# First token group of a convolution and MLP kernel: exponential, block B, doubling copy and wake-up moved

## Chip, core and metric

The kernel runs on one core of one Trainium2 chip. The metric is device microseconds of one execution, as the median of several runs. The core has five engines that run side by side: TensorE (matmuls; PE in the profile, its weight loads PEld), VectorE (DVE), ScalarE (ACT), GpSimd (POOL) and SyncE (SP). SyncE only issues transfers (DMA). ScalarE and GpSimd can issue them too, each on a queue of its own, in program order with their other instructions.

## The reference

A dynamic convolution over 16384 tokens (4 sequences of 4096) with 192 features, 8 heads and 7 taps, followed by an MLP with a squared Relu:

```python
w = np.exp(weight_gen - max over the 7 taps)
w = w / (w.sum over the 7 taps + 1e-09)
x_pad = six rows of zeros ahead of each sequence, then x
conv[b, s, h, :] = sum over k of w[b, s, h, k] * x_pad[b, s + k, h, :]
h = conv @ w_in                  # 192 -> 2048
r = np.maximum(h, 0.0)
g = s * (r * r) + b
out = g @ w_out                  # 2048 -> 192
```

## The kernel before, in words

The tokens go in 32 groups of 512. The 2048 hidden features are 16 blocks of 128, handled in pairs as eight chunks; `wc_91` to `wc_98` are the eight converted weight chunks in the listings (chunks 0 to 7 here).

Precision: float32 values are split into a high part in a reduced format (fp32r) and the rest. Products are made of high x high, low x high and high x low, so a group's operands are `xa` and `xb` (two blocks of the 192 features), each with a high half `[:, 0]` and a low half `[:, 1]`. `xb` fills only 64 partitions, and is copied once to the other 64 (the doubling copy, `xb<-xb`), since the matmuls use both halves.

Weights: `load_weights` (L167) brings chunk pairs from DRAM: four transfers of block A (L179), eight small ones of block B (L188) and one of the second weights (L196) per chunk. For the first pair chunk 0 and chunk 1 are loaded by calls of their own. `convert(i)` (L209) splits a chunk in steps, between which other work stands: ScalarE takes Abs (L218, needs the whole raw chunk); VectorE makes three passes (L221, L225, L229); ScalarE casts the high part (L234, reads L229's result); VectorE makes `v` (L236, L240); TensorE adds up six matmuls (L250 to L252), and ScalarE casts the low part (L253). `ahead(i, n)` runs the next n steps of chunk i.

The first group of the program has a convolution of its own (`conv_pieces`, g == 0): softmax of the taps (`softmax_a` L370 on VectorE, `exp` L382 on ScalarE, `softmax_b` L385 on VectorE), then products of `xr` (the group's rows of x) with `w`: the "row tails" (eight products that end in `xb`) and the "row firsts" (eight that end in `xa`). TensorE transposes and sums the products into PSUM (`px`, L320): 28 for the tails, 28 for the firsts. `row_hi` (L353) casts the high half on ScalarE, `row_lo` (L359) makes the low half on VectorE and, for `xb`, issues the doubling copy (L364). `run_pieces(0, a, b)` runs pieces a to b of that list.

TensorE's start: `awake` (L258) runs 48 small matmuls on constants while the first data is fetched. Then come the transposes, and `mm1_pair` (L512) makes the first products of chunk 0: six each of `xa` and `xb`, with the rest of chunk 0's conversion between them.

The order of instructions is written out by hand (`tc.manual_schedule`): each engine runs its own in the order of the program text. Transfers of SyncE and ScalarE count their completion on eight semaphores that they share in turn; a transfer that takes a semaphore again first waits until the one before it on that semaphore has landed. After the first group (from L708) the loop over the other 31 groups keeps TensorE full with `mm1_quad` and `mm2_quad`.

Of the kernel before, what the change touches and what calls it, by code (L numbers as in the profile page):

```python
# [20 lines left out]
def dynamic_conv_then_relu2_mlp(  # L21
# [24 lines left out]
    nc = tc.nc  # L46
# [3 lines left out]
    P = 128  # L50
# [43 lines left out]
    def load_rows(i):  # L94

        t0 = ORDER[i] * T
        wg = xin.tile([P, NT, H, K], F32, tag="wg", name="wg")
        nc.sync.dma_start(
            out=wg.rearrange("p a h k -> p (a h k)"),
            in_=wgf[t0:t0 + T, :].rearrange("(p a) n -> p (a n)", a=NT),  # L100
        )
        xt = rows.tile([P, NT + HALO, D], F32, tag="xr", name="xr")
        src = xf[t0 - HALO:t0 - HALO + 1, :]
        for a0, a1 in ((0, 2 * NT - 1), (2 * NT - 1, NT + HALO)):
            nc.sync.dma_start(
                out=xt[:, a0:a1].rearrange("p a d -> p (a d)"),
                in_=bass.AP(src.tensor, src.offset + a0 * D, [[NT * D, P], [1, (a1 - a0) * D]]),
            )
        xt_t[i], wg_t[i] = xt, wg
# [99 lines left out]
    def convert(i):  # L209


        r = raw_t[i // 2][:, i % 2]
        hi, lo = wc[i][:, 0], wc[i][:, 1]
        low_w, high_w = r[:, :, 0], r[:, :, 1]
        fv = high_w.bitcast(F32)
        t = raw.tile([P, CW], U32, tag="t", name="t", bufs=1)
        tv = t.bitcast(F32)
        nc.scalar.activation(out=tv, in_=fv, func=AF.Abs)  # L218
        yield

        nc.vector.tensor_scalar(  # L221
            out=tv, in0=tv, scalar1=LEAST, scalar2=MOST, op0=ALU.max, op1=ALU.min
        )

        nc.vector.tensor_scalar(  # L225
            out=t, in0=t, scalar1=3, scalar2=0x3FFFFFFF,
            op0=ALU.logical_shift_left, op1=ALU.bitwise_and,
        )
        nc.vector.scalar_tensor_tensor(  # L229
            out=high_w, in0=high_w, scalar=0xC0000000, in1=t,  # L230
            op0=ALU.bitwise_and, op1=ALU.bitwise_or,
        )
        yield
        nc.scalar.copy(out=hi, in_=fv)  # L234

        nc.vector.tensor_scalar(  # L236
            out=t, in0=high_w, scalar1=0xFF800000, scalar2=None, op0=ALU.bitwise_and
        )
        v = raw.tile([P, CW], F32R, tag="v", name="v", bufs=2)
        nc.vector.scalar_tensor_tensor(  # L240
            out=v, in0=low_w, scalar=2.0 ** -52, in1=tv, op0=ALU.mult, op1=ALU.mult
        )
        yield

        ps = ps_h.tile([P, 2, T], F32, tag="h1", name="ph")
        n = CW // 2
        for a in range(2):
            c = slice(a * n, (a + 1) * n)
            o = ps[:, a, 0:n]
            nc.tensor.matmul(out=o, lhsT=eye_f, rhs=fv[:, c], start=True, stop=False)  # L250
            nc.tensor.matmul(out=o, lhsT=neg_eye, rhs=hi[:, c], start=False, stop=False)  # L251
            nc.tensor.matmul(out=o, lhsT=eye, rhs=v[:, c], start=False, stop=True)  # L252
        nc.scalar.copy(out=lo.rearrange("p (a n) -> p a n", a=2), in_=ps[:, :, 0:n])  # L253
        yield
# [3 lines left out]
    def awake():  # L258

        ph = ps_h.tile([P, 2, T], F32, tag="h1", name="ph")  # L260
        for _ in range(48):
            nc.tensor.matmul(out=ph[:, 0, 0:P], lhsT=eye, rhs=ones, start=True, stop=True)  # L262

    def constants():
        nc.gpsimd.memset(ones_f, 1.0)
        nc.vector.tensor_copy(out=ones, in_=ones_f)
        nc.gpsimd.affine_select(
            out=eye_f, in_=ones_f, pattern=[[-1, P]], base=0, channel_multiplier=1,
            compare_op=ALU.is_equal, fill=0.0,
        )  # L270
        nc.vector.tensor_copy(out=eye, in_=eye_f)
        nc.vector.tensor_scalar(
            out=neg_eye, in0=eye_f, scalar1=-1.0, scalar2=None, op0=ALU.mult
        )
# [29 lines left out]
    def conv_pieces(g):  # L304
# [33 lines left out]
        def row_firsts(k0, k1):  # L338
            def f():
                out = st["p"][0][:, k0:k1].rearrange("p k a (q n) -> p k (a q) n", q=Q)  # L340
                times(out[:, :, :, 0:G], 0, k0, k1 - k0, 0, NT * Q, 2, G)
                times(out[:, :, :, G:32], G, k0, k1 - k0, 0, NT * Q, 2, 32 - G)
                for a in range(NT):
                    sum_taps(0, k0, k1, a)
            return f
# [10 lines left out]
        def row_lo(i):  # L356
            def f():
                x = st["x"][i]
                nc.vector.tensor_tensor(  # L359
                    out=x[R[i], 1], in0=st["ps"][i][R[i]], in1=x[R[i], 0].bitcast(F32), op=ALU.subtract  # L360
                )
                if i == 1:
                    b = x.bitcast(F32)
                    nc.sync.dma_start(out=b[P // 2:P], in_=b[0:P // 2])  # L364
                else:
                    xt_t.pop(g)
                    x_t[g] = parts_of(st["x"])
            return f
# [97 lines left out]
        if g == 0:  # L466
            return [
                softmax_a, exp, softmax_b, row_tails(0), row_tails(1), row_tails(2), row_tails(3), row_hi(1),
                row_lo(1), row_firsts(0, 2), row_firsts(2, 4), row_firsts(4, 6), row_firsts(6, 7),
                row_hi(0), row_lo(0),  # L470
            ]
        return [
# [39 lines left out]
    def mm1_pair(n, p, between=None):  # L512

        g, k = divmod(n, NQ)
        new_h(n, p, "h0")
        turns = [(0, (0, 1, 2)), (1, (0, 1, 2))] if between is None else [
            (0, (0, 2)), (1, (0, 2)), (0, (1,)), (1, (1,))
        ]
        left = 6
        for at, (block, cs) in enumerate(turns):  # L520
            if at == 2:
                between()
            for c in cs:
                part, v = x_t[g][block][c]
                left -= 1
                for j, rows in enumerate(HALVES[::-1]):
                    rows = rows if block else slice(0, P)
                    nc.tensor.matmul(  # L528
                        out=h_t[n, p][:, j], lhsT=w1(2 * k + p, part, block, j, rows), rhs=v[rows],
                        start=(at == 0 and c == 0), stop=(left == 0),  # L530
                    )
# [121 lines left out]

    with tc.manual_schedule():
        constants()
        load_rows(0)
        nc.scalar.activation(out=spare, in_=ones_f[:, 0:1], func=AF.Exp)
        load_weights(0, (0,), nc.scalar)
        load_weights(0, (1,))
        load(1)  # L660
        load_weights(1)
        nc.sync.dma_start(out=s_sb, in_=s.partition_broadcast(P))
# [6 lines left out]
                next(parts[i])  # L669

        awake()
        run_pieces(0, 0, 7)
        ahead(0, 1)
        run_pieces(0, 7, 8)
        ahead(0, 1)
        run_pieces(0, 8, 15)
        ahead(0, 1)
        ahead(1, 1)

        beside = ((2, 4), (4, 5), (5, 7), (7, 8), (8, 10), (10, 12), (12, 14), (14, 15))  # L680
# [84 lines left out]
```

## Time and profile before

| | |
|---|---|
| median of 3 runs | 1195.92 us (1195.82 to 1199.31) |
| the profiled execution | 1195.58 us, its span 1193.9 us |
| mean granted TensorE clock over the span | 0.994 |
| busy over the span: TensorE, weight loads, VectorE, ScalarE, GpSimd | 1172.4, 1052.6, 931.9, 825.6, 6.1 us |

Times below count from the span's start. A busy TensorE is one with a matmul in flight, not one at its peak. Transfer issues on a queue (SPq, ACTq) are listed by the time that the issuing took, waits included where they fall between merged issues; when the data has landed is in another view. The granted clock is a share of 2.4 GHz.

### The profile page before, as it was taken

The numbers are of one execution on the slowest core, as the hardware profiler recorded it, in microseconds if no ns is written. First come the engines' busy times: TensorE is split into PE (matmuls) and PEld (weight loads), VectorE is DVE, ScalarE is ACT, GpSimd is POOL, SyncE is SP. The second block draws the span as 40 slices with busy tenths as digits, with TensorE's granted clock in tenths as the row PEclk, the third lists the DMA queues.
The fourth block names the chain that finished last, engine by engine and source line by source line (L and its number), as shares of the span: only waits on it lengthen the run. The fifth ranks groups of instructions, "written<-read, shape, count | busy, mean of one in ns | idle before, by whom it ended". The sixth has DMA issues, their size and how long they took to land.

```text
span 1193.9 us, 30070 instructions
## 1 busy us (share of the span) xinstructions
PE 1172.4 (98%) x12776; PEld 1052.6 (88%) x12776; DVE 931.9 (78%) x1356; ACT 825.6 (69%) x890; POOL 6.1 (1%) x22
## 2 busy tenths in 40 slices
PE   7799999999999999999999999999999999999997
PEld 6578899998999989999899898998989989899897
DVE  5788777788877778887777887777888777888843
ACT  1676677776776767767677676776767767677674
POOL 0000000000000000000000000000000000000000
PEclk9899999999999999999999999999999999999999
DMA  6332222211222221222221222222112222212110
GB/s 148 99 60 41 46 45 33 46 26 34 46 45 44 34 45 25 36 45 46 33 45 28 35 43 46 46 32 46 26 34 46 46 41 37 41 28 37 24 23 15
DMA packets 171370, 50.63 MB, mean 42 GB/s; under 512 B 160228, under 2 KB 163940, under 8 KB 171236
## 3 DMA queue, kind: packets, MB, share of 16 engines
q1 hardware_dynamic: 170980, 48.58, 23.7%
q8 instruction: 100, 1.64, 0.6%
q14 instruction: 34, 0.28, 0.1%
q10 hardware_dynamic: 256, 0.13, 0.0%
HBM read 27.70 MB, written 12.58 MB: 34 GB/s over the span
## 4 chain that ended last, share of the span: by engine, by line
PE 96%; DVE 1%; ACT 1%; DMA 0%; issue 0%; POOL 0%; ACTq 0%; POOLq 0%
PE po L615 47%; PE ph L546 43%; PE po L597 2%; PE ph L528 1%; PE ph L262 1%; PE px L320 1%; PE ph L250 1%; DVE gl L569 0%; DMA xb<-xb 0%; ACT gh L563 0%; ACT r L559 0%; ACT r L557 0%; PE ph L285 0%; PE ph L252 0%; PE ph L251 0%
## 5 line engine op out<-in xcount | busy, mean ns | idle before, releaser
L615 PE MATMUL po<-wc,gh 64*128 64x384 f32 x3936 | 570.8, 356 | 0.0
L615 PE MATMUL po<-wc,gl 64*128 64x192 f32 x3936 | 493.5, 247 | 0.7 <-DVE gl L569 0.7
L569 DVE TENSOR_TENSOR gl<-r,gh 128x1024 fp32r<-128x1024 f32 x256 | 313.0, 1223 | 221.5 <-ACT gh L563 213.1
L557 ACT ACTIVATE r<-ph 128x1024 f32<-128x1024 f32 x256 | 248.8, 1023 | 308.6 <-PE ph L546 303.7
L615 PEld LDWEIGHTS po<-wc,gl 64*128 64x128 f32 x3936 | 375.7, 188 | 6.2 <-DVE gl L569 1.0
L615 PEld LDWEIGHTS po<-wc,gh 64*128 64x128 f32 x3936 | 369.2, 184 | 5.5
L546 PE MATMUL ph<-xa,wc 64*128 64x512 f32 x2976 | 371.0, 394 | 0.0
L546 PEld LDWEIGHTS ph<-xa,wc 64*128 64x128 f32 x2976 | 269.6, 184 | 57.3 <-issue 0.2
L563 ACT CAST gh<-r 128x1024 fp32r<-128x1024 f32 x256 | 268.8, 1050 | 7.9
L559 ACT ACTIVATE r<-r 128x1024 f32<-128x1024 f32 x256 | 271.1, 1059 | 0.3
L546 PE MATMUL ph<-xb,wc 64*128 64x512 f32 x1488 | 193.0, 391 | 0.0
L406 DVE TENSOR_TENSOR pr<-xt,w 128x1536 f32<-128x1536 f32 (+1 forms) x124 | 187.5, 1553 | 1.8 <-DVE w L392 0.6
L546 PEld LDWEIGHTS ph<-xb,wc 64*128 64x128 f32 x1488 | 139.5, 184 | 34.1
L417 DVE TENSOR_TENSOR pr<-pr 128x1536 f32<-128x1536 f32 (+1 forms) x124 | 140.7, 1154 | 2.1
L627 DVE SCALAR_TENSOR_TENSOR u<-po,s_sb,bias 128x192 f32<-128x192 f32 x128 | 49.7, 408 | 1.6 <-PE po L597 1.6
L633 DVE SCALAR_TENSOR_TENSOR y<-po,s_sb,u 128x192 f32<-128x192 f32 x128 | 49.6, 408 | 0.1
L425 DVE TENSOR_TENSOR acc<-pr 128x768 f32<-128x768 f32 x31 | 29.7, 958 | 1.1
L436 DVE STREAM_TRANSPOSE xT<-acc 128x128 f32<-128x128 f32 x124 | 27.6, 280 | 1.0
L441 DVE STREAM_TRANSPOSE xT<-acc 128x128 f32<-128x128 f32 x124 | 26.3, 269 | 0.0
L597 PE MATMUL po<-wc,gh 128*128 128x384 f32 x80 | 24.0, 362 | 0.1
L597 PE MATMUL po<-wc,gl 128*128 128x192 f32 x80 | 20.4, 254 | 1.9 <-DVE gl L569 1.9
L454 DVE TENSOR_TENSOR xa<-xT,xa 128x512 fp32r<-128x512 f32 x31 | 21.2, 684 | 0.0
(55 smaller groups left out, 360.0 us busy)
## 6 DMA issues: line engine op xcount, KB each, us to landing
xt<-in_x_dram SPq DMA_DIRECT2D x120, 132.0 KB, 4.0
out_dram<-y SPq DMA_DIRECT2D x124, 96.0 KB, 1.9
xb<-xb SPq DMA_DIRECT2D x124, 64.0 KB, 2.3
wg<-in_weight_gen_dram SPq DMA_DIRECT2D x124, 28.0 KB, 2.6
r<-in_moe_w_out_dram SPq DMA_DIRECT2D x8, 384.0 KB, 3.7
r<-in_moe_w_in_dram SPq DMA_DIRECT2D x12, 128.0 KB, 2.8
r<-in_moe_w_in_dram SPq DMA_DIRECT2D x24, 32.0 KB, 2.6
xr<-in_x_dram SPq DMA_DIRECT2D x1, 672.0 KB
```

What stands on the lines that cost most here:

```text
L406: nc.vector.tensor_tensor(out=pr[:, k0:k1, :, h * G:(h + 1) * G], in0=bass.AP(xs.tensor, xs.offset, [xs.ap[0], [FQ, n], [FQ, J], [1, G]]), ...
L417: nc.vector.tensor_tensor(out=pr[:, o:o + n], in0=pr[:, o:o + n], in1=pr[:, a:a + n], op=ALU.add)
L425: nc.vector.tensor_tensor(out=acc, in0=pr[:, 0], in1=pr[:, 2], op=ALU.add)
L546: nc.tensor.matmul(out=h_t[n, p][:, j], lhsT=w1(2 * k + p, part, block, j, rows), rhs=v[rows], start=(at < 2 and c == 0), stop=(at >= 4 an ...
L557: nc.scalar.activation(out=r[p], in_=h_t.pop((n, p)), func=AF.Relu)
L559: nc.scalar.activation(out=r[p], in_=r[p], func=AF.Square)
L563: nc.scalar.copy(out=gh, in_=r[p])
L569: nc.vector.tensor_tensor(out=gl, in0=sq, in1=gh.bitcast(F32), op=ALU.subtract)
L597: nc.tensor.matmul(**m)
L615: nc.tensor.matmul(**m)
L627: nc.vector.scalar_tensor_tensor(out=u[i], in0=o_t[g][tiles[i]][:, 1, :], scalar=s_sb, in1=bias, op0=ALU.mult, op1=ALU.add,)
L633: nc.vector.scalar_tensor_tensor(out=y[:, t], in0=o_t[g][t][:, 0, :], scalar=s_sb, in1=u[i - 1], op0=ALU.mult, op1=ALU.add,)
```

## The change

Five edits, all in the first 50 us:

- The dummy exponential on `spare`, which loads ScalarE's table, stands ahead of `load_rows(0)`.
- Block B of chunks 0 and 1 (16 transfers of 16 KB) is issued from GpSimd; before, chunk 0's eight were ScalarE's and chunk 1's eight SyncE's.
- The doubling copy of `xb` is issued from ScalarE, not SyncE.
- `awake` runs four float32 matmuls on `wg` (224 columns), not 48 on constants, and so waits for `wg` to land.
- Order of the first group: the cast of the high weights stands one step earlier; `row_firsts(0, 2)` stands ahead of `row_lo(1)`; the last `ahead` of chunk 0 ahead of `row_lo(0)`; and the products with a high x high part of both blocks stand ahead of the conversion, the other eight behind it.

```diff
         )
+        nc.scalar.copy(out=hi, in_=fv)
         yield
-        nc.scalar.copy(out=hi, in_=fv)
...
         ph = ps_h.tile([P, 2, T], F32, tag="h1", name="ph")
-        for _ in range(48):
-            nc.tensor.matmul(out=ph[:, 0, 0:P], lhsT=eye, rhs=ones, start=True, stop=True)
+        w = wg_t[0].rearrange("p a h k -> p (a h k)")
+        for _ in range(4):
+            nc.tensor.matmul(out=ph[:, 0, 0:NT * H * K], lhsT=eye_f, rhs=w, start=True, stop=True)
...
-                    nc.sync.dma_start(out=b[P // 2:P], in_=b[0:P // 2])
+                    nc.scalar.dma_start(out=b[P // 2:P], in_=b[0:P // 2])
...
-                row_lo(1), row_firsts(0, 2), row_firsts(2, 4), row_firsts(4, 6), row_firsts(6, 7),
+                row_firsts(0, 2), row_lo(1), row_firsts(2, 4), row_firsts(4, 6), row_firsts(6, 7),
...
-            (0, (0, 2)), (1, (0, 2)), (0, (1,)), (1, (1,))
+            (0, (0,)), (1, (0,)), (0, (2, 1)), (1, (2, 1))
...
         constants()
+        nc.scalar.activation(out=spare, in_=ones_f[:, 0:1], func=AF.Exp)
         load_rows(0)
-        nc.scalar.activation(out=spare, in_=ones_f[:, 0:1], func=AF.Exp)
-        load_weights(0, (0,), nc.scalar)
-        load_weights(0, (1,))
+        load_weights(0, (0,), nc.gpsimd)
+        load_weights(0, (1,), nc.gpsimd)
...
         awake()
-        run_pieces(0, 0, 7)
+        run_pieces(0, 0, 2)
         ahead(0, 1)
-        run_pieces(0, 7, 8)
+        run_pieces(0, 2, 8)
         ahead(0, 1)
-        run_pieces(0, 8, 15)
+        run_pieces(0, 8, 14)
         ahead(0, 1)
+        run_pieces(0, 14, 15)
         ahead(1, 1)
```

ScalarE, from its first instruction to the cast of chunk 0's low weights; before, then with the change (`e` is the softmax's input, `r` a raw weight chunk, `t` its absolute value, `px` the transposed sums):

```order
L657 ACT_TABLE_LOAD
L657 ACTIVATE spare<-ones_f 128x1
L188 DMA r<-in_moe_w_in_dram 16x256 x8
L383 ACTIVATE e<-e 128x224
L218 ACTIVATE t<-r 128x768
L353 CAST xb<-px 64x512
L353 CAST xa<-px 128x512
L234 CAST wc_91<-r 128x768
L218 ACTIVATE t<-r 128x768
L253 CAST wc_91<-ph 128x768
```

```order
L657 ACT_TABLE_LOAD
L657 ACTIVATE spare<-ones_f 128x1
L384 ACTIVATE e<-e 128x224
L218 ACTIVATE t<-r 128x768
L354 CAST xb<-px 64x512
L233 CAST wc_91<-r 128x768
L365 DMA xb<-xb 64x1024
L354 CAST xa<-px 128x512
L218 ACTIVATE t<-r 128x768
L253 CAST wc_91<-ph 128x768
```

The eight transfers ahead of the exponential are gone, the cast of the high weights has moved ahead of xa's, and the doubling copy stands between the two. The second Abs is chunk 1's, ahead of the cast L253 of chunk 0 in both.

VectorE, from the row tails to the first pass over chunk 1 (`pr` are the products, `w` the softmax); before, then with the change:

```order
L310 TENSOR_TENSOR pr<-xr,w 128x7x2x16 x8
L221 TENSOR_SCALAR t<-t 128x768
L225 TENSOR_SCALAR t<-t 128x768
L229 SCALAR_TENSOR_TENSOR r<-r,t 128x768
L359 TENSOR_TENSOR xb<-px,xb 64x512
L310 TENSOR_TENSOR pr<-xr,w 128x32x24
...
L359 TENSOR_TENSOR xa<-px,xa 128x512
L236 TENSOR_SCALAR t<-r 128x768
L240 SCALAR_TENSOR_TENSOR v<-r,t 128x768
L221 TENSOR_SCALAR t<-t 128x768
```

```order
L311 TENSOR_TENSOR pr<-xr,w 128x7x2x16 x8
L221 TENSOR_SCALAR t<-t 128x768
L225 TENSOR_SCALAR t<-t 128x768
L229 SCALAR_TENSOR_TENSOR r<-r,t 128x768
L311 TENSOR_TENSOR pr<-xr,w 128x32x24
L311 TENSOR_TENSOR pr<-xr,w 128x32x8
L360 TENSOR_TENSOR xb<-px,xb 64x512
...
L236 TENSOR_SCALAR t<-r 128x768
L240 SCALAR_TENSOR_TENSOR v<-r,t 128x768
L360 TENSOR_TENSOR xa<-px,xa 128x512
L221 TENSOR_SCALAR t<-t 128x768
```

Two row firsts now stand ahead of xb's low half, and `v` ahead of xa's.

TensorE, from the wake-up to the second chunk's conversion; before, then with the change:

```order
L262 MATMUL ph<-ones,eye 128x128 x48
L320 MATMUL px<-eye_f,pr 64x128 x28
L320 MATMUL px<-eye_f,pr 128x128 x28
L528 MATMUL ph<-xa,wc_91 128x512 x4
L528 MATMUL ph<-xb,wc_91 128x512 x4
L250 MATMUL ph<-r,eye_f 128x384
...
L528 MATMUL ph<-xa,wc_91 128x512 x2
L528 MATMUL ph<-xb,wc_91 128x512 x2
```

```order
L263 MATMUL ph<-wg,eye_f 128x224 x4
L321 MATMUL px<-eye_f,pr 64x128 x28
L321 MATMUL px<-eye_f,pr 128x128 x28
L529 MATMUL ph<-xa,wc_91 128x512 x2
L529 MATMUL ph<-xb,wc_91 128x512 x2
L250 MATMUL ph<-r,eye_f 128x384
...
L529 MATMUL ph<-xa,wc_91 128x512 x4
L529 MATMUL ph<-xb,wc_91 128x512 x4
```

Four products instead of eight stand ahead of the conversion (L250 and the five behind it), eight instead of four behind it.

## Rows read from the trace of the kernel before

**Rows 1.** Stretches: from:to, length, busy us (instructions) of PE, PEld, DVE, ACT, POOL, clock, DMA, GB/s.

```profile
0.00:17.00 17.00, 15.27 (x73) 14.47 (x74) 7.25 (x20) 2.78 (x4) 0.76 (x6) 1.00 0.49 146
17.00:33.00 16.00, 6.64 (x37) 5.62 (x35) 11.11 (x19) 2.83 (x4) 0.00 (x0) 0.81 0.80 169
...
95.00:1180.00 1085.00, 1084.26 (x12312) 981.89 (x12310) 860.03 (x1242) 773.79 (x830) 5.30 (x16) 1.00 0.23 37
```

**Rows 2.** Chain of waits, 0 to 60 us: start us, us, what.

```profile
20.12 4.93 PE px L320 x28
...
25.07 0.59 ACT xa L353
...
29.27 4.67 DMA xb<-xb
...
33.98 1.22 PE ph L528 x4
35.20 1.58 PE ph L250 x2
...
38.42 0.05 ACT wc L253
...
49.17 2.37 PE po L597 x15
```

**Rows 3.** Waits, 0 to 50 us: us in total, times, longest us.

```profile
PE ph L528 <- DMA xb<-xb: 6.3, 1, 6.3
```

**Rows 4.** Timeline: start us, us, instruction, [idle before it, what ended that].

```profile
1.05 1.32 ACTq L188 DMA_DIRECT2D r<-in_moe_w_in_dram  x3
1.08 0.34 POOL L267 TENSOR_SCALAR_AFFINE_SELECT eye_f<-ones_f 128x128 f32<-128x128 f32 x1
...
2.40 5.98 ACTq L188 DMA_DIRECT2D r<-in_moe_w_in_dram  x5
...
3.38 0.39 DVE L377 TENSOR_TENSOR e<-wg,mx 128x224 f32<-128x224 f32 x1
8.42 0.39 ACT L383 ACTIVATE e<-e 128x224 f32<-128x224 f32 x1 [6.12 <-DMA r<-in_moe_w_in_dram]
...
10.29 2.50 DVE L310 TENSOR_TENSOR pr<-xr,w 128x224 f32<-128x224 f32 x8
11.10 3.66 SPq L188 DMA_DIRECT2D r<-in_moe_w_in_dram  x8
...
12.28 0.90 ACT L218 ACTIVATE t<-r 128x768 f32<-128x768 f32 x1 [3.47 <-DMA r<-in_moe_w_in_dram]
...
14.41 0.96 DVE L229 SCALAR_TENSOR_TENSOR r<-r,t 128x768 uint32<-128x768 uint32 x1
...
18.18 0.68 DVE L359 TENSOR_TENSOR xb<-px,xb 64x512 fp32r<-64x512 f32 x1 [2.82 <-ACT xb L353]
18.79 4.35 DVE L310 TENSOR_TENSOR pr<-xr,w 128x768 f32<-128x768 f32 x8
...
26.88 0.96 DVE L240 SCALAR_TENSOR_TENSOR v<-r,t 128x768 fp32r<-128x768 uint32 x1
...
39.89 0.90 ACT L218 ACTIVATE t<-r 128x768 f32<-128x768 f32 x1
```

**Rows 5.** SyncE's own waits, 0 to 50 us: us in total, times, longest us.

```profile
SPq L179 <- DMA xr<-in_x_dram: 4.4, 1, 4.4
```

**Rows 6.** Weight loads by shape, 0 to 55 us: busy us, mean ns, idle before.

```profile
L262 PEld LDWEIGHTS ph<-ones,eye 128*128 128x128 f32 x48 | 10.3, 332 | 1.7 <-DVE eye L271 1.7
...
L528 PEld LDWEIGHTS ph<-xa,wc 128*128 128x128 f32 x18 | 3.1, 188 | 4.1 <-ACT wc L253 2.1 <-ACT wc L234 1.7
```

**Rows 7.** DMA issues, 0 to 60 us: count, KB each, median us to landing.

```profile
r<-in_moe_w_out_dram SPq DMA_DIRECT2D x6, 384.0 KB, 3.7
...
r<-in_moe_w_in_dram ACTq DMA_DIRECT2D x8, 16.0 KB, 4.9
r<-in_moe_w_in_dram SPq DMA_DIRECT2D x8, 16.0 KB, 1.9
```

## The prediction

> **What bounds the kernel now.** I read the stretches first. In the long middle (95 to 1180 us) TensorE is busy 1084.26 of 1085 us, so nothing but its own work sets the time there [rows 1], and none of that work is edited. In 17 to 33 us it is busy 6.64 of 16. A gain can only come from the first 50 us, and whatever starts the continuous TensorE work earlier shortens the whole kernel by as much.
>
> Then the chain of waits through that start [rows 2]. It runs through the wake-up, the transposes of the first group, and the doubling copy of xb (4.67 us); only then come the products, the conversion matmuls of chunk 0 and, at 38.42, the copy L253 that ends this conversion. I call that moment T. From T on ScalarE's order is the same in both kernels, so I count everything up to T.
>
> The waits name the biggest hole: TensorE waits 6.3 us for xb<-xb [rows 3]. Its issue at 29.27 is late because it stands at the end of SyncE's list, although VectorE had finished xb at 18.86 [rows 2, 4]. The second hole is earlier. ScalarE issues eight 16 KB transfers before the exponential; these take from 1.05 to 8.38, so the exponential starts at 8.42 though its input was ready at 3.77 [rows 4]. SyncE itself stands 4.4 us in the middle of chunk 0's weights, waiting for xr [rows 5].
>
> The clock: the view prints 1.00 for the first 17 us [rows 1], but a 128x128 weight load takes 332 ns in the wake-up against 188 ns in the products [rows 6]. I therefore take the lower level (1.2 GHz) for the wake-up: its 48 matmuls did not bring the higher one while they ran.
>
> **The change, part by part**, against the profiled execution (1195.58 us, span 1193.9; the median of the runs shown is 1195.92, which is 0.34 more).
>
> *Exponential.* It can start at 3.8. From its start in the trace to the first row tail is 1.87 us (8.42 to 10.29), so the tails could start at 5.7 [rows 4]. They then wait for xr, which landed by 10.3 at the latest (in the trace they waited for nothing). With their 2.50 us they end between 8.2 and 12.8.
>
> *Block B on GpSimd.* No row shows a GpSimd transfer. The nearest row is the same eight transfers from ScalarE, 7.3 us or 0.92 us each [rows 4]. The lower bound is SyncE's eight in 3.66 us, 0.46 each; for the upper I let each issue cost a whole issue-to-landing of 16 KB, 1.9 us [rows 4, 7]. I take 0.92. GpSimd is free at 1.42, so chunk 0's eight are issued by 8.8; with 2.6 us to land (between 1.9 and 4.9 [rows 7]) they are there at 11.4, and chunk 1's eight at 18.7 (1.4 + 16 x 0.92 + 2.6). The Trainium skill ("DMA: Bandwidth & Descriptors", Specifications) gives about 1 us to the first byte for this path against 0.6 for the other two. With 1 us per issue, an estimate from that page, everything below would come 0.6 us later; no run here shows it.
>
> *SyncE's list.* It loses eight block-B issues (3.66 us) and the doubling copy. SyncE's and ScalarE's transfers share eight completion semaphores, and a ninth waits until the one before it on its semaphore has landed. With block B gone, wg, two parts of xr, four of block A and chunk 0's second weights are just eight: of the 4.4 us stall nothing stays ahead of them. The last is issued near 4 instead of behind the stall, lands by 9 with 4.9 us, and does not decide. Chunk 0 begins at 11.4 (12.28 in the trace).
>
> *From chunk 0 to T.* Abs L218 to the end of L229: 3.1 us as in the trace (12.28 to 15.37) [rows 4], so 14.5 (15.0 if the tails end at 12.8). VectorE then does the eight firsts (4.35) with xb's low part (0.6) behind the second: 19.5. The first two took 1.3 (18.79 to the transposes' start at 20.12 [rows 2, 4]), so xb is ready at 16.4. TensorE's last four transposes (4.93 / 28 = 0.18 each [rows 2]) end at 20.2, ScalarE's xa copy (0.6) at 20.8; beside it VectorE makes v (L236 and L240, the longer 0.96) by 21.4 [rows 2, 4]. The hi copy L234 is now earlier on ScalarE, behind L229, hidden by the firsts. Then four products instead of eight stand before the conversion, 1.22 / 4 = 0.3 each [rows 2]: 22.0. The conversion itself takes 3.2 (35.20 to 38.42 [rows 2], mostly at the lower clock). **T = 25.2 instead of 38.42: 13.2 us less.**
>
> *Doubling copy on ScalarE.* Issued at about 16.4, when VectorE has xb, it lands at 21.1 if it keeps its 4.67, and is wanted at 21.4. It is hidden by the firsts and the xa copy, with 0.3 us of cover; without it each us late costs a us. Behind it on ScalarE stands only the xa copy, which starts 3.8 us later.
>
> *Wake-up.* Four float32 matmuls of 224 columns, once wg has landed, before 3.4. The pair L250 of 384 columns took 1.58 [rows 2], so each is at most 0.92 and all end by 7.1, where the 48 end at about 12 (1.7 + 10.3 [rows 6]). The tail transposes, paced by the tails or at 0.18 each, then end by 13 at the latest. The xb copy (0.6) that waits for them stands behind Abs (ends 12.3) and its reader runs at 15.7: hidden, over 2 us of cover. If the clock rises sooner, the conversion saves up to half of its 3.2.
>
> *Order of the products.* Four more products stand behind T. Two (xa's low part) run while L253 works; the others may delay the first Relu by 0 to 0.5 us. I take 0.
>
> *Chunks 1 to 3.* Abs of chunk 1 would run at 21.4; its data is there at 18.7, 2.7 us of cover. Chunk 2 is wanted 1.5 us behind T (39.89 against 38.42 [rows 2, 4]), at 26.7. SyncE had issued it before the doubling copy at 29.3 [rows 2], and its list gets 8.1 us shorter (3.66 + 4.4): 21.2 at the latest, and with 3.7 us to land [rows 7] 24.9, 1.8 us of cover.
>
> Sum: 13.2 us off 1195.58 is 1182.4, and against the median **1182.7 us**.
>
> **The rivals.**
>
> *GpSimd is slow (slower).* Abs of chunk 1 stands ahead of L253 on ScalarE. With p us per issue chunk 1 is complete at 1.4 + 16p + 2.6, and Abs adds 0.9. T passes 38.42 once p is over 2.1 us. At 2.5 T is 44.9 and the time 1202. For it: no row prices this queue. Against it: 2.1 is more than any whole 16 KB transfer of SyncE's took, by the median [rows 7]. Chance 0.06.
>
> *GpSimd in between (no change).* From p = 1.9 to 2.3 the result lies within 3.6 us of before, 0.3%, about what a measurement can tell from no change; at 1.9 T is 35.3 and the time 1192.8. Chance 0.07.
>
> *GpSimd's issues stop while VectorE works (still faster).* In the trace GpSimd has nothing to do beside VectorE here, so nothing speaks against it. The tails' 2.50 us [rows 4] then delay chunk 0 to 13.9. Some four of chunk 1's issues fit into VectorE's wait for Abs, the other four follow when v is made at 21.4 + 2.5 = 23.9: chunk 1 at 23.9 + 3.7 + 2.6 = 30.2, Abs ends at 31.1, so 7.3 us gained instead of 13.2: 1188.6. The Trainium skill has such a rule, against this change ("SBUF — State Buffer", SBUF: two separate sides): GpSimd cannot write descriptors while VectorE runs in a mode that takes both ports, and it advises the other queues. By that page the tails, which read two tensors, would not do it, and the short L221 and L236 would; no row here shows either. Chance 0.12.
>
> *The transfers are the bound (still faster).* In 17 to 33 us the transfer engines are 0.80 busy [rows 1]. If the work only crowds and chunk 2 lands at 33.0 as now (29.3 + 3.7) instead of 24.9, Abs of chunk 2 starts then instead of at 39.89: 6.9 gained, 1189.0. For it: the landings of up to 4.9 us under load [rows 7]. Against it: the queues leave holes that now close. Chance 0.15.
>
> **How the numbers follow.** The forecast keeps 0.60. Its own range: p = 0.46 brings chunk 0 forward to about 9 (its other weights), T to 22.8 and the time to 1180.3; half of the 1.6 us that a sooner clock could give takes it to 1179.5. p = 1.3 puts chunk 0 at 14.4, T at 28.2, 1185.7. The range over the cases goes from 1179.5 to 1191.0: it takes in both rivals near 1189, with 2 us above the later one for landings that run longer than I took, and leaves out the two slow-GpSimd ones (0.13). Faster 0.87, within 0.3% 0.07, slower 0.06.
>
> **What would show it.** Right: the exponential near 3.8; GpSimd issues of about 0.9 us; Abs of chunk 0 near 11.4; xb<-xb issued near 16.4 and no TensorE wait of over 1 us for it; L253 near 25; the stretch behind it, from L253 to the first second-layer product, as long as before (10.75 us, 38.42 to 49.17 [rows 2]). Wrong: Abs of chunk 0 or 1 waiting for GpSimd's transfers beyond 20; Abs of chunk 2 waiting for SyncE's; GpSimd's issues spread out between VectorE's instructions; or the 10.75 us growing, which would mean that the start was ready and the gain is given back behind T.

## The result, and the profile after

The changed kernel takes **1185.09 us** (median of 4 runs, 1184.21 to 1185.39) against 1196.12 for the kernel before beside it: ratio 0.9901, 95% interval 0.9883 to 0.9918. That is 11.0 us less; 13.2 were predicted. The profiled execution took 1185.39 us, its span 1183.7 (before: 1195.58 and 1193.9). Lines from the first cast of the conversion on count one higher than before (L364 is now L365, L597 is L598).

The timeline of the changed kernel, with the instructions that answer to [rows 4] (start, us, instruction, idle before it and what ended that):

```profile
1.48 3.98 POOL L188 DMA_DIRECT2D r<-in_moe_w_in_dram  x8
...
3.74 0.39 ACT L384 ACTIVATE e<-e 128x224 f32<-128x224 f32 x1 [1.43 <-DVE e L378]
...
7.36 1.90 DVE L311 TENSOR_TENSOR pr<-xr,w 128x224 f32<-128x224 f32 x6 [0.53 <-DMA xr<-in_x_dram]
...
11.80 0.89 ACT L218 ACTIVATE t<-r 128x768 f32<-128x768 f32 x1 [7.68 <-DMA r<-in_moe_w_in_dram]
...
16.07 0.68 DVE L360 TENSOR_TENSOR xb<-px,xb 64x512 fp32r<-64x512 f32 x1
16.21 5.74 PE L321 MATMUL px<-eye_f,pr 128*128 128x128 f32 x28 [5.62 <-DVE pr L311]
16.67 3.15 DVE L311 TENSOR_TENSOR pr<-xr,w 128x768 f32<-128x768 f32 x6
16.78 0.50 ACTq L365 DMA_DIRECT2D xb<-xb  x1
...
21.98 0.58 ACT L354 CAST xa<-px 128x512 fp32r<-128x512 f32 x1 [6.12 <-PE px L321]
22.31 3.58 SPq L188 DMA_DIRECT2D r<-in_moe_w_in_dram  x8
...
25.93 0.94 SPq L196 DMA_DIRECT2D r<-in_moe_w_out_dram  x2
26.05 0.80 ACT L253 CAST wc<-ph 128x768 fp32r<-128x768 f32 x1 [2.68 <-PE ph L252]
...
29.33 0.89 ACT L218 ACTIVATE t<-r 128x768 f32<-128x768 f32 x1 [1.69 <-issue]
...
38.60 0.36 PE L598 MATMUL po<-wc,gl 128*128 128x192 f32 x1 [1.15 <-DVE gl L570]
```

Read it at three points. T, the start of L253, is 26.05 instead of 38.42: 12.37 us gained, 13.2 predicted. The Abs of chunk 2 (the second L218 shown) starts at 29.33 instead of 39.89: 10.56 gained. The first second-layer product that waits for gl is at 38.60 instead of 49.17: 10.57 gained. So 1.8 us are given back between T and chunk 2's Abs, where both kernels run the same ScalarE order; behind that Abs nothing more is lost up to the product. Before, the Abs followed T by 1.47 without a wait; here by 3.28, with a wait of 1.69 in it.

What stands behind that wait shows in SyncE's own waits (us in total, times, longest). The 4.4 us of [rows 5] in chunk 0's weights are gone, and this stands first:

```profile
SPq L188 <- DMA xb<-xb: 5.2, 1, 5.2
```

Between 17.12 and 22.31 SyncE issued nothing: block B of chunks 2 and 3 waited for the landing of the doubling copy, which is on *ScalarE's* queue and whose data those weights have nothing to do with. In the built program every transfer of SyncE and ScalarE adds to one of eight semaphores, handed out in turn over both queues, and a transfer waits until the earlier one on its semaphore has landed. The trace's records of the issues name them: the copy has semaphore 104, its turn lying between those of SyncE's first two `xt` transfers (103 and 105), and the next transfer with 104 is the first of block B of chunks 2 and 3. Moving the copy to the other queue did not take it out of that ring. Chunk 2's second weights, behind the eight block-B issues, then went out at 25.93. The last count on their semaphore comes at 29.11; ScalarE's wait for it, which began at 26.14, ends at 29.14, and the Abs starts at 29.33. The chain of waits (start, us, what) goes through the same place:

```profile
16.16 0.60 DVE xb L360
16.78 5.51 DMA xb<-xb
22.31 0.31 SPq L188
...
25.93 0.42 SPq L196
...
27.42 3.58 DMA b_sb<-in_moe_b_dram
...
38.60 2.37 PE po L598 x15
```

(`b_sb` stands in this chain for 0.27 us that VectorE idled before a pass over chunk 2. They cost nothing: the product follows the Abs by 9.27 us here and by 9.28 before.)

TensorE's 6.3 us of waiting for xb [rows 3] are gone; the copy, landed at 22.29, is hidden by the xa copy. The other thing to see is the clock. In stretches of the changed kernel (from:to, length, busy us of PE, PEld, DVE, ACT, POOL, granted clock, DMA share, GB/s):

```profile
14.00:16.00 2.00, 0.00 (x0) 0.00 (x0) 2.00 (x3) 0.88 (x1) 0.00 (x0) 0.60 0.89 149
16.00:18.00 2.00, 1.79 (x8) 1.57 (x8) 2.00 (x5) 0.00 (x0) 0.00 (x0) 0.50 1.23 197
18.00:20.00 2.00, 2.00 (x11) 2.00 (x11) 2.00 (x5) 0.00 (x0) 0.00 (x0) 0.50 1.10 223
20.00:22.00 2.00, 1.95 (x12) 1.71 (x11) 1.25 (x2) 0.01 (x1) 0.00 (x0) 0.70 0.31 63
```

TensorE has nothing to do for 5.62 us ahead of the firsts' transposes, the clock falls to the lower level (1.2 GHz), and the 28 transposes run at it: 5.74 us, ending 2.1 us behind VectorE's last first (21.95 against 19.82). The transfer engines are 0.89 and more busy from 2 to 20 us (the view's share can come out above 1).

And GpSimd's issues (ns min/median/max of one, then issue to landing):

```profile
L188 POOL DMA_DIRECT2D r<-in_moe_w_in_dram x16: 484/484/640, 1.5 to 11.6; - x16
...
DMA to landing us min/median/max: 3.7/5.0/6.3
```

### The profile page after: what moved, and what is told of

It reads as the page before. It is cut to its first block, busy times and chain, and to the rows that moved or that the text cites. A ratio compares the mean times of both kernels' runs of the same rounds, so it can differ in the third digit from the quotient of the medians.

```text
span 1183.7 us, 30013 instructions
## 1 busy us (share of the span) xinstructions
PE 1163.2 (98%) x12736; PEld 1043.1 (88%) x12736; DVE 932.2 (79%) x1356; ACT 825.6 (70%) x890; POOL 13.9 (1%) x38
## 4 chain that ended last, share of the span: by engine, by line
PE 95%; DMA 1%; DVE 1%; ACT 1%; issue 0%; SPq 0%; POOL 0%; DVEq 0%; POOLq 0%
PE po L616 47%; PE ph L547 44%; PE po L598 2%; PE ph L529 1%; DMA r<-in_moe_w_in_dram 1%; PE ph L250 1%; DMA xb<-xb 0%; DVE gl L570 0%; DMA b_sb<-in_moe_b_dram 0%; SPq L188 0%; ACT gh L564 0%; POOL r L188 0%; PE ph L286 0%; ACT r L560 0%; ACT r L558 0%
## 5 line engine op out<-in xcount | busy, mean ns | idle before, releaser
L598 PE MATMUL po<-wc,gh 128*128 128x384 f32 x80 | 24.0, 362 | 0.1
L598 PE MATMUL po<-wc,gl 128*128 128x192 f32 x80 | 20.4, 254 | 2.0 <-DVE gl L570 2.0
L455 DVE TENSOR_TENSOR xb<-xT,xb 128x512 fp32r<-128x512 f32 x31 | 21.2, 685 | 0.0
```

The source lines that it names most:

```text
L598: nc.tensor.matmul(**m)
```

## The experiments

Every kernel below was timed against the kernel before on its own chip (medians 1196.5 to 1197.15 there). T and "Abs 2" (chunk 2's Abs) are from each profiled execution.

| kernel | T | Abs 2 | span | span - Abs 2 | median | ratio, 95% interval |
|---|---|---|---|---|---|---|
| before | 38.42 | 39.89 | 1193.9 | 1154.0 | 1196.12 | |
| the change | 26.05 | 29.33 | 1183.7 | 1154.4 | 1185.09 | 0.9901, 0.9883 to 0.9918 |
| xb_gpsimd | 25.85 | 27.33 | 1181.8 | 1154.5 | 1184.24 | 0.9890, 0.9876 to 0.9903 |
| xb_sync | 32.97 | 34.45 | 1188.7 | 1154.2 | 1190.91 | 0.9947, 0.9934 to 0.9961 |
| warm | 25.25 | 29.59 | 1183.8 | 1154.2 | 1185.69 | 0.9909, 0.9894 to 0.9925 |
| warm_xb_gpsimd | 26.13 | 27.62 | 1182.3 | 1154.7 | 1183.47 | 0.9882, 0.9869 to 0.9896 |
| awake48 | 27.01 | 28.62 | 1183.0 | 1154.4 | 1184.90 | 0.9902, 0.9888 to 0.9915 |
| blockb_sync | 27.27 | 34.45 | 1189.2 | 1154.8 | 1190.74 | 0.9951, 0.9938 to 0.9965 |
| xr_last | 25.64 | 27.14 | 1182.0 | 1154.9 | 1183.71 | 0.9890, 0.9877 to 0.9904 |
| warm2 | 26.39 | 27.88 | 1182.5 | 1154.6 | 1183.87 | 0.9893, 0.9879 to 0.9906 |
| before_xb_scalar | 28.42 | 32.40 | 1186.6 | 1154.2 | 1188.54 | 0.9932, 0.9920 to 0.9945 |
| before_exp_blockb | 30.97 | 32.46 | 1186.7 | 1154.2 | 1189.28 | 0.9948, 0.9934 to 0.9961 |
| old_order | 28.25 | 30.26 | 1184.7 | 1154.4 | 1186.35 | 0.9914, 0.9900 to 0.9927 |
| xr_later | 28.44 | 29.94 | 1184.4 | 1154.5 | 1185.79 | 0.9912, 0.9899 to 0.9926 |

The fifth column is the main finding: in all 14 kernels the span is the start of chunk 2's Abs plus 1154.0 to 1154.9. T is not such a point: span less T runs from 1155.5 to 1161.9. Chunk 2's Abs starts at the later of two times: T + 1.5 (L253 and one cast go before it on ScalarE; in old_order 2.0, as VectorE's v comes late), or 0.2 us behind the landing of chunk 2's second weights, the last of its transfers on SyncE's list. The views name that landing in blockb_sync alone; in the change, warm and before_xb_scalar they put the wait down to "issue". The semaphore counts in the traces settle it: the last count for those weights comes at 29.11 in the change, 29.36 in warm, 32.17 in before_xb_scalar, 34.23 in blockb_sync and 28.40 in awake48, and the Abs follows by 0.22 or 0.23 us in all five. In the other nine it comes before T. The kernels differ in which of the two decides.

### The doubling copy on GpSimd's queue (xb_gpsimd)

```diff
-                    nc.scalar.dma_start(out=b[P // 2:P], in_=b[0:P // 2])
+                    nc.gpsimd.dma_start(out=b[P // 2:P], in_=b[0:P // 2])
```

> The changed kernel with the doubling copy xb<-xb issued from GpSimd, whose transfers count on semaphores of their own. Theory S (shared semaphore): in the changed kernel the copy on ScalarE holds one of the eight semaphores that SyncE's next transfer needs, SyncE stands 5.2 us, chunk 2's weights land late, Abs of chunk 2 runs at 29.3 instead of 27.6, and the stretch from L253 to the first second-layer product is 12.55 us instead of 10.75. So here: no SyncE wait over 1 us for xb, the stretch 10.7 to 10.9, time 1183.3 (1.8 less than 1185.1). Rival C (crowding): chunk 2 is late because the transfer engines are full; SyncE's wait goes but the stretch stays at 12 or more, time 1185. Under both, TensorE waits for xb only if the copy takes more than 6.4 us from its issue near 16.8.

GpSimd's transfers have eight semaphores of their own (110 to 117 in the trace), so this takes the copy out of SyncE's ring and leaves it off SyncE's list. The timeline:

```profile
16.94 4.22 SPq L188 DMA_DIRECT2D r<-in_moe_w_in_dram  x8
16.97 0.53 POOL L365 DMA_DIRECT2D xb<-xb  x1 [4.97 <-DVE xb L360]
...
21.21 1.30 SPq L196 DMA_DIRECT2D r<-in_moe_w_out_dram  x2
...
25.85 0.80 ACT L253 CAST wc<-ph 128x768 fp32r<-128x768 f32 x1 [2.65 <-PE ph L252]
27.33 0.90 ACT L218 ACTIVATE t<-r 128x768 f32<-128x768 f32 x1
```

Block B starts to go out 5.4 us earlier, just ahead of the copy's issue, and the second weights at 21.21 instead of 25.93. Chunk 2's Abs follows T by 1.48 without a wait, and the span is 1.9 us shorter. This settles what the 1.8 us were: with rival C the stretch behind L253 would have stayed at 12 us or more, and it is 11.0 (10.7 to 10.9 expected). The median is 0.85 below the change's, inside both intervals, and 0.9 above the expected 1183.3: the traces show the gain, the times alone would not.

### The doubling copy back on SyncE (xb_sync)

```diff
-                    nc.scalar.dma_start(out=b[P // 2:P], in_=b[0:P // 2])
+                    nc.sync.dma_start(out=b[P // 2:P], in_=b[0:P // 2])
```

> The changed kernel with the doubling copy alone put back on SyncE, at the end of its list. It is issued when the list is through, near 22.7, and lands near 27.4; TensorE's products of xb wait for it (23.3 in the changed kernel), so L253 moves from 26.05 to about 30.2. SyncE no longer stands for it, so the stretch behind L253 is 10.8 again: first second-layer product near 41.0 instead of 38.6, time 1187.5. If the copy was hidden anyway (rival), L253 stays near 26 and the time is 1183 to 1185.

The timeline:

```profile
23.47 0.55 SPq L365 DMA_DIRECT2D xb<-xb  x1
...
28.25 0.80 PE L529 MATMUL ph<-xb,wc 64*128 64x512 f32 x2 [4.29 <-DMA xb<-xb]
...
32.97 0.80 ACT L253 CAST wc<-ph 128x768 fp32r<-128x768 f32 x1 [8.96 <-PE ph L252]
```

The 6.3 us of [rows 3] come back as 4.29: the copy stands at the end of a now shorter list. T and the time are later than I expected (30.2 and 1187.5): in the 4.29 us without work the granted clock fell again (0.71 in 24 to 28 us, 0.56 in 29 to 33), and the conversion took 4.0 us (28.97 to 32.97) instead of 2.35. The edit is worth 5.8 us by the medians here, 5.0 by the spans.

### Block B of chunks 0 and 1 back on SyncE (blockb_sync)

```diff
-        load_weights(0, (0,), nc.gpsimd)
-        load_weights(0, (1,), nc.gpsimd)
+        load_weights(0, (0,))
+        load_weights(0, (1,))
```

> The changed kernel with block B of chunks 0 and 1 issued by SyncE at the same place of the program. Theory (the queue that issues is the lever: SyncE's list gets 8 us longer, all that stands behind it comes later): the Abs of chunk 0 starts about 14 us instead of 11.80, xr lands as before or later, L253 starts 2 to 3 us later, and block B of chunk 2 lands 5 us or more later still; time 1188 to 1190. Rival (the transfer engines, busy from 2 to 20 us in the changed kernel, are the bound, and the queue gives back issue time alone): the last bytes land when they did, L253 within 0.7 us of 26.05, time under 1186.

The timeline:

```profile
27.27 0.80 ACT L253 CAST wc<-ph 128x768 fp32r<-128x768 f32 x1 [2.68 <-PE ph L252]
...
34.45 0.89 ACT L218 ACTIVATE t<-r 128x768 f32<-128x768 f32 x1 [5.59 <-DMA r<-in_moe_w_out_dram]
```

The queue is the lever, but not where I looked for it. Chunk 0's Abs is only 1.4 later (13.19) and T only 1.2 (2 to 3 expected); the prediction followed GpSimd's issues to exactly these. The loss (5.5 us of the span; the median is 0.7 above the expected range) is in the second row: SyncE's list, 16 issues longer, lands chunk 2's second weights at 34.23. Block B's move pays mostly because of what it clears *off SyncE*, not because of when it lands itself. The list holds a wait for the copy here too, in front of an `xt` transfer; how much of the 5.5 us it accounts for, no run separates. SyncE's own waits (us in total, times, longest):

```profile
SPq L139 <- DMA xb<-xb: 2.3, 1, 2.3
```

### The old wake-up (awake48)

```diff
-            nc.tensor.matmul(out=ph[:, 0, 0:NT * H * K], lhsT=eye_f, rhs=w, start=True, stop=True)
+            nc.tensor.matmul(out=ph[:, 0, 0:P], lhsT=eye, rhs=ones, start=True, stop=True)
```

(48 of the second instead of 4 of the first.)

> The changed kernel with the old wake-up of 48 products. In the changed kernel the new wake-up's clock was full from 6.84 to 13.67 us and half after it. Theory (the wake-up is worth what it gives the tails' transposes): without it the clock rises only some microseconds into steady transposing, the four tails' transposes end 2 to 4 us later, the low half of xb follows them at 18 instead of 16.07, L253 starts 1.5 to 2.5 us later than 26.05, and the time is 1186.5 to 1187.5. Rival (hidden, as the prediction had it, which put more than 2 us of cover there): L253 within 0.5 us, time within 0.4 us of 1185.1.

The timeline:

```profile
18.21 0.68 DVE L359 TENSOR_TENSOR xb<-px,xb 64x512 fp32r<-64x512 f32 x1 [1.86 <-ACT xb L353]
...
20.16 2.74 PE L320 MATMUL px<-eye_f,pr 128*128 128x128 f32 x20 [1.71 <-DVE pr L310]
...
24.78 0.94 SPq L196 DMA_DIRECT2D r<-in_moe_w_out_dram  x2
...
27.01 0.80 ACT L253 CAST wc<-ph 128x768 fp32r<-128x768 f32 x1 [2.63 <-PE ph L252]
...
28.62 0.90 ACT L218 ACTIVATE t<-r 128x768 f32<-128x768 f32 x1
```

Its wait of SyncE for the copy:

```profile
SPq L188 <- DMA xb<-xb: 4.0, 1, 4.0
```

(The granted clock left its higher level at about 14.4 us in the changed kernel, not at 13.67: it was 1.00 in 12 to 14 us and 0.60 in 14 to 16.) Neither theory holds whole (the rival has the time right and T wrong): the tails' transposes (in the chain of waits 28 from 12.25, 5.33 us) end 7 us later than in the changed kernel and xb's low half is 2.1 us later (VectorE waits 1.86 for it), but T moves by only 0.96, and Abs 2 is even 0.71 earlier (28.62); the median does not move. Three things give it back. The late transposes (0.19 us each, where the changed kernel's 28 took 3.70) end just ahead of the firsts, so there is no long hole, the firsts' transposes run at 0.137 each, and they end 0.9 us behind VectorE instead of 2.1. The changed kernel had 1.7 us of waiting behind T to spare. And the copy's turn in the ring came two transfers later here (semaphore 106, not 104): two transfers of block B went out ahead of SyncE's wait, the wait was 4.0 us instead of 5.2, and the second weights went out at 24.78 instead of 25.93. The new wake-up brings the hole forward along with the work.

### Work in the hole (warm, warm_xb_gpsimd, warm2)

```diff
         run_pieces(0, 2, 8)
+        warm(11)
         ahead(0, 1)
```

(warm(n): n products like the wake-up's, never read. warm_xb_gpsimd adds the copy on GpSimd; warm2 has that too, with 13 here and one more behind each of two groups of the firsts.)

> The changed kernel with 11 more dummy matmuls of the wake-up's kind between the tail transposes and the first transposes (TensorE idles there from 10.6 to 16.2). Theory K (clock): the granted clock falls in that hole, so the 28 transposes of the firsts take 5.74 us, 0.2 each, and end 2.1 us behind VectorE's last product. Here the clock stays high, they end near 20.4 instead of 21.95, L253 starts near 24.5 instead of 26.05. With theory S the time does not move (1185.1, within 0.4), since Abs of chunk 2 waits for its weights until 29.3 all the same and the stretch behind L253 grows to 14. Without S the whole 1.5 us comes through: 1183.6.

> Both edits together: the doubling copy on GpSimd and 11 dummy matmuls in TensorE's hole. With S and K both gains come through: L253 near 24.5, the stretch behind it 10.8, first second-layer product near 35.3 instead of 38.6, time 1181.8. With S alone 1183.3; with K alone (no S) 1183.6; with C 1185. Possible loss: chunk 2's second weights would have to land by 26.

> The changed kernel with the doubling copy on GpSimd, 13 products without a use in the gap of TensorE before the firsts' transposes, and one more behind each of two groups of them, so that the clock isn't lost there (with 11 and none later it held in one kernel and fell at 17.92 in the other). Theory (the last transposes ended 2.1 us behind VectorE because the clock was half): granted clock full from 7 to 26, the last transposes end 0.5 to 1 us behind VectorE's last pass, L253 starts at 24.7 to 25.3, time 1182.5 to 1183.3 against 1184.24 for the copy alone. Rival (VectorE's passes or the scheduling of the products bound the stretch, and the clock costs nothing): L253 within 0.4 us of 25.85, time 1184 or more.

The timeline of warm:

```profile
18.41 2.73 PE L329 MATMUL px<-eye_f,pr 128*128 128x128 f32 x20 [0.70 <-DVE pr L319]
...
25.25 0.80 ACT L253 CAST wc<-ph 128x768 fp32r<-128x768 f32 x1 [2.63 <-PE ph L252]
29.59 0.89 ACT L218 ACTIVATE t<-r 128x768 f32<-128x768 f32 x1 [2.74 <-issue]
```

The clock stays at its higher level (1.00 from 14 to 24 us), the last transposes end at 21.14, and T is 0.8 earlier (1.5 expected) although chunk 0's Abs was 0.4 later; the whole of it goes into a longer wait (2.74) for chunk 2, as theory S has it. With the copy on GpSimd that wait is gone, and the two ways of holding the clock should show. They did not: in warm_xb_gpsimd's profiled execution the clock fell all the same (0.63 granted in 18 to 20 us, 0.52 in 20 to 22) and T is 26.13. (Its other three executions, with a mean clock of 0.999 to 1.000 over the span against 0.997 in this one, took 1182.20 to 1183.77 us against 1184.00; they have no trace.) In warm2 it held from 12 to 24 us, T is 26.39 (24.7 to 25.3 expected), and the filler itself stood in the way, as its timeline shows:

```profile
13.38 5.08 PE L264 MATMUL ph<-wg,eye_f 128*128 128x224 f32 x26
...
18.30 1.04 PE L329 MATMUL px<-eye_f,pr 128*128 128x128 f32 x8
```

The thirteen products (26 passes) hold TensorE until 18.30, where the first transposes could have begun at 16.2. So the clock costs 0.8 us of T or somewhat more here, shown by the profiled execution of warm alone, and neither version that was tried gains it safely: both medians lie within half a microsecond of each other and 0.4 to 0.8 below xb_gpsimd, inside its interval, and above what was expected (1181.8, and 1182.5 to 1183.3).

### xr behind the weights (xr_last, xr_later)

```diff
-        load_rows(0)
-        load_weights(0, (0,), nc.gpsimd)
+        load_rows(0, lambda: load_weights(0, (0,), nc.gpsimd))
         load_weights(0, (1,), nc.gpsimd)
```

(load_rows calls the function between wg and xr. The copy is on GpSimd. xr_later calls it for chunk 1 too, and has xb's low half one group of firsts later.)

> The changed kernel with the doubling copy on GpSimd and chunk 0's weights issued by SyncE ahead of the big transfers of xr instead of behind them (the program that GpSimd and ScalarE issue is the same but for the copy). Its neighbour with the copy alone took 1184.24. Theory (GpSimd's small transfers landed 5 us and more after their issue because the megabyte ahead of them held the transfer engines): the first of GpSimd's lands before 5, the eighth at 8 to 9 instead of 11.3, the Abs of chunk 0 starts at 8.5 to 9.5 instead of 11.80, xr and with it the tails come about 2 us later, and the time is 1182.5 to 1184. Rival (those 5 us belong to the path of GpSimd's queue): the first still lands at 6.3, the eighth at about 11, the Abs within 0.7 us of 11.80, and the time is 1184 to 1186 by the later tails.

> The kernel with the doubling copy on GpSimd and xr behind chunk 0's weights, with xr now behind chunk 1's weights as well, and the low half of xb one group of firsts later. In its neighbour, five of GpSimd's eight transfers for chunk 0 were issued ahead of xr or beside it and landed 2 to 3.3 us after their issue, three behind it landed 5.4 to 6.4 us after. Theory (place in time against the megabyte decides the landing, not the queue): now all eight land 2 to 4 us after their issue, the last by 9.5, the Abs of chunk 0 starts by 10 instead of 11.86; xr lands about 2 us later than there and VectorE does the conversion ahead of the tails. Time 1182 to 1184 (what is gained in front can be lost by the tails). Rival (GpSimd's path has a latency of its own of some 5 us, or its first five were early by chance): the last of the eight still at 11 or later, Abs at 11.5 or later, time over 1184.

In xr_last GpSimd's transfers that were issued before SyncE sent xr (at 3.63 and 4.15), five of the eight, landed 2.0 to 3.7 us after their issue; the three behind it took 5.4 to 6.4, and since chunk 0 needs all eight its Abs moved by nothing (11.86). That the time, 1183.71, lies in the theory's range is therefore no support for it. In xr_later xr is issued at 6.02, all eight land within 2.0 to 4.2 us and chunk 0 is complete at 9.0. The timeline of xr_later:

```profile
9.52 0.89 ACT L219 ACTIVATE t<-r 128x768 f32<-128x768 f32 x1 [5.33 <-DMA r<-in_moe_w_in_dram]
...
13.39 0.69 DVE L312 TENSOR_TENSOR pr<-xr,w 128x224 f32<-128x224 f32 x2 [7.75 <-DMA xr<-in_x_dram]
```

Same queue, same issues, and the Abs is 2.3 us earlier: the theory holds that the place against the 960 KB of xr decides the landing, not a latency of GpSimd's path. It does not pay (1185.79, where 1182 to 1184 was expected), because the tails then start at 13.39 instead of 6.14 and, against what I had expected, still stand ahead of the conversion on VectorE: T 28.44.

### One part alone on the kernel before (before_xb_scalar, before_exp_blockb)

before_xb_scalar has the copy on ScalarE and nothing else:

> The kernel before with one edit alone: the doubling copy on ScalarE's queue. Theory (the copy stood behind SyncE's list and was the last thing the first products waited for): it is issued at about 18.9 instead of 29.3 and lands by 24, the products follow xa at 26 instead of 33.98, the clock of that stretch stays uncertain, L253 starts at 30 to 32 instead of 38.42. Block B of chunk 2 comes no earlier than before, as SyncE's list is as long, so that part of the 6 to 8 us is lost behind L253; time 1189 to 1192 (6 to 8 us less at most). Rival (SyncE's list is the bound behind L253, so the copy alone gives almost nothing): time 1195 to 1196 although L253 is earlier.

Its timeline:

```profile
17.69 0.54 ACTq L364 DMA_DIRECT2D xb<-xb  x1
...
28.42 0.80 ACT L253 CAST wc<-ph 128x768 fp32r<-128x768 f32 x1 [1.84 <-PE ph L252]
32.40 0.89 ACT L218 ACTIVATE t<-r 128x768 f32<-128x768 f32 x1 [2.38 <-issue]
```

T is better than I expected (30 to 32), and so is the time: the granted clock was 1.00 in 17 to 33 us in this execution, where [rows 1] has 0.81; why it did not fall here, no run shows. Chunk 2 waits, as expected, for its second weights (issued at 28.52): of the 10.0 us at T 7.5 are left at Abs 2, and 8.0 by the medians. SyncE does not wait for the copy in this kernel: it comes to the copy's semaphore (105) at 25.25, when the copy has landed (21.95).

before_exp_blockb moves the exponential and block B and leaves the copy on SyncE:

> The kernel before with the other two edits of queues alone: the exponential ahead of ScalarE's transfers, block B of chunks 0 and 1 on GpSimd; the doubling copy stays on SyncE, the order of work and the wake-up stay. Theory (the parts need each other: the copy stays last, but SyncE's list in front of it is 7 to 8 us shorter): exponential at 3.7, Abs of chunk 0 at about 12, copy issued at 22 to 24 and landed by 28.5, L253 at 32 to 33.5, time 1190 to 1191.5, near the 1190.91 of the changed kernel with its copy on SyncE. Rival (the gain comes from the rows' early products, whatever the copy does): L253 at 27 to 28, time under 1187.5.

Its timeline:

```profile
24.75 0.55 SPq L364 DMA_DIRECT2D xb<-xb  x1
...
27.92 0.73 PE L528 MATMUL ph<-xb,wc 64*128 64x512 f32 x4 [0.59 <-DMA xb<-xb]
...
30.97 0.80 ACT L253 CAST wc<-ph 128x768 fp32r<-128x768 f32 x1 [2.56 <-PE ph L252]
```

The copy is issued later than expected but lands 3.1 us after that, not 4.7, so T is 1 to 2.5 us ahead of the expectation; chunk 2 follows it without a wait. The median, 1189.28, is 0.7 below the expected range, but the five runs go from 1188.28 to 1192.14. Alone the two parts bring Abs 2 forward by 7.5 and 7.4 us, together (with wake-up and order) by 10.6: each shortens the way to the first products. In the first kernel the late second weights then set Abs 2; in the second TensorE still waits 0.59 us for the copy, and what else keeps T at 30.97 no run takes apart.

### The old order (old_order)

```diff
-                row_firsts(0, 2), row_lo(1), row_firsts(2, 4), row_firsts(4, 6), row_firsts(6, 7),
+                row_lo(1), row_firsts(0, 2), row_firsts(2, 4), row_firsts(4, 6), row_firsts(6, 7),
...
-            (0, (0,)), (1, (0,)), (0, (2, 1)), (1, (2, 1))
+            (0, (0, 2)), (1, (0, 2)), (0, (1,)), (1, (1,))
```

(With the pieces' ranges and the hi cast as in the kernel before.)

> The changed kernel with the old order of the pieces (tails ahead of chunk 0's Abs, xb's low half ahead of the first two firsts, the conversion's cast behind its yield, the products' old turns); queues and wake-up stay changed. Theory (VectorE waits for xb's cast with nothing to do, about 1 us, and the products come later by some tenths; but block B of chunk 2 holds the stretch behind L253, with 1.7 us between L253's path and that data): L253 0.8 to 2 us later than 26.05, time 1184.5 to 1186. Rival (the order is a lever of its own): time over 1187.

The timeline:

```profile
28.25 0.80 ACT L253 CAST wc<-ph 128x768 fp32r<-128x768 f32 x1 [1.86 <-PE ph L252]
30.26 0.90 ACT L218 ACTIVATE t<-r 128x768 f32<-128x768 f32 x1 [0.42 <-DVE v L240]
```

T is 2.2 later, a little more than the expectation's upper end, and Abs 2 is 0.93 later; the median, 1186.35, is 0.35 above the range I gave. More than half of the 2.2 us that the new order gives at T is lost again in the changed kernel's wait for chunk 2.

## Why the prediction was right, and where it was not

It said faster, 1182.7 with 1179.5 to 1191.0; 1185.09 came. That T came within 0.85 us of the forecast is in part luck: twice, two errors cancel. By its steps:

- **Exponential:** 3.8 predicted, 3.74 measured; tails ended by 9.26, inside 8.2 to 12.8.
- **Block B on GpSimd:** two terms were mis-sized, and that they cancelled is luck. An issue costs 0.48 to 0.50 us, near the lower bound (SyncE's 0.46) and not ScalarE's 0.92, whose row held waits (its first three took 1.32 us, 0.44 each). Landing takes 5.0 by the median, not 2.6. Chunk 0's Abs came at 11.80 against 11.4. The 1.9 us of [rows 7] was SyncE's price once the big transfers had landed; xr_last and xr_later show that it is the crowd, and in both GpSimd's shortest landing is 2.0. The Trainium skill's 1 us against 0.6 ("DMA: Bandwidth & Descriptors", Specifications) is a time to the first byte, not the price of an issue that the prediction made of it; its difference of 0.4 us is too small to see beside landings of 2.0 to 6.4.
- **From chunk 0 to T:** 25.2 predicted, 26.05 measured. VectorE ended its firsts at 19.82 (19.5), but the last transposes ended 2.1 us behind it, where 0.7 were allowed, four of them at 0.18. The rows of before already had 1.9 there (25.05 against 23.14 [rows 2, 4]): at the lower clock the transposes fall behind VectorE, so that more than four are left. Where the clock was up they end 0.9 behind it (warm, awake48). On the other side the conversion took 2.35 (23.70 to 26.05) instead of 3.2, because by then the clock was up.
- **Doubling copy:** issued 16.78 (16.4), landed 22.29 (21.1), and still hidden, as the xa copy was later too. That only the xa copy stands behind it on ScalarE was true of the queue and missed the semaphores.
- **Wake-up:** "hidden, over 2 us of cover" is wrong at T by 0.96 (awake48) and right in the time, with the help of the ring.
- **Order of the products:** 0 to 0.5 us; where chunk 2 does not wait (xb_gpsimd) the stretch from L253 to the gl product is 11.0 instead of 10.75.
- **Chunks 1 to 3: the step that failed.** It gave chunk 2 "1.8 us of cover", from SyncE's list alone. Of the list it was right: in xb_gpsimd, where nothing holds it, chunk 2's second weights go out at 21.21 and have landed at 24.74, against 21.2 and 24.9 in the forecast. In the changed kernel SyncE came to block B at 17.12 and stood there 5.2 us for the copy, the weights went out at 25.93 and landed at 29.11, and cover turned into a wait of 1.7 us. I had used the ring of eight for chunk 0 and did not go round it for chunk 2, although the copy was a transfer that the change itself moved in it. The sign that I had set for this, the 10.75 us growing, is what the trace shows: 12.55.

12.4 at T less 1.8 makes the 10.6 seen at the first gl product; 0.4 of that is lost later in the span of the profiled executions, which no run took apart.

Of the rivals, *slow GpSimd* and *in between* fell with the issue price. *The transfers are the bound* was half right: the engines are full to 20 us and set when chunk 0 lands, but not the time. That *GpSimd's issues stop while VectorE works* was not seen: beside the tails each took 0.48 us, as elsewhere. The longest, 0.64, is the first (at 1.48), beside VectorE's short casts L272 and L273; whether they lengthened it or its being the first, no run shows. The Trainium skill's rule on the shared port ("SBUF — State Buffer", SBUF: two separate sides) stays untested for L221 and L236: chunk 1's last issue began at 11.6, and the first L221 at 12.73.

## What to carry to other kernels

When a transfer moves to another queue, follow its completion semaphore as well as its queue: who waits for the slot that it now holds, and what stands behind that waiter. Look for the one instruction whose start, plus a constant, gives the time in every variant (here chunk 2's Abs), and count gains there; a gain at an earlier point is only worth what the other input of that instruction lets through. And expect parts of one change to overlap: two that bring 7.5 and 7.4 us alone brought 10.6 together with the rest.

## What the hardware showed that was not expected

- Small transfers landed when the big ones ahead of them were through, on both queues seen: GpSimd's 16 KB took 2.0 us at the least (xr_last) and up to 6.3 in the changed kernel, behind xr, where SyncE's 64 KB transfers of block A took 5.8 by the median.
- Four float32 products of the wake-up had the tails' 28 transposes run in 3.70 us in the changed kernel; behind the 48 products they took 5.33. In blockb_sync, xb_sync and warm2, with the same four, they took 5.34, 5.49 and 5.36: when the higher level comes is not the same in every execution.
- A GpSimd issue took 0.48 us, as good as SyncE's 0.46.
- Work put into an idle stretch to hold the clock held it in the profiled execution of two of three kernels, and in one of those it delayed the work that the clock was for.
- The same copy held SyncE for 5.2 us in the changed kernel, for 4.0 in awake48 and not at all in before_xb_scalar, by the place of its turn in the ring and by when SyncE came to that turn again.
